# Block sums left in PSUM for the router's products, and all low weight parts of a layer made by GpSimd

## The chip, the cores and the metric

The kernel runs on one core of a Trainium2 chip. The metric is the device time of one execution in microseconds; lower is better. TensorE multiplies matrices into PSUM, VectorE and ScalarE read and write SBUF and PSUM, GpSimd works on SBUF, and SyncE (SP) issues most of the transfers.

## The reference

Linear attention feeds two layers of experts. In the attention, `q` is a softmax over its 64 columns, `k` one over the 576 rows, and the output is `q (kᵀ v)` for 8 batches of 8 heads; its rows, 4608 tokens of 512 columns, go through the two layers.

```python
def _moe_ref(x, w_skip, w_gate, w1, w2):           # first layer
    do_compute = x @ w_skip > 0
    xc = x[do_compute]; logits = xc @ w_gate
    e_idx = argmax(logits, 1); gate_w = softmax(logits)[e_idx]
    y[e] = gate_w * (relu(xc[e] @ w1[e]) @ w2[e])  # for the rows of each of 8 experts
    out[do_compute] = xc + y                       # the other rows pass unchanged
def _moe2_ref(x, emb, tau, w1, w2):                # second layer, all rows
    logits = (x / |x|) @ (emb / |emb|).T / tau
    e_idx = argmax(logits, 1); gate_w = softmax(logits)[e_idx]
    out[e] = gate_w * (relu(x[e] @ w1[e]) @ w2[e])
```

`w1` is 512x1024 and `w2` 1024x512 for each expert, in float32.

## The kernel before

The attention (up to about 200 us) ends with each token's first router; each row is scattered by an indirect DMA to a DRAM table X, sorted by expert. A plan (`Plan`, small vectors on one partition) turns the counts of rows into steps. A step is two blocks of 128 rows of one expert, or a single block at the end of an expert with an odd number of blocks. Class `Moe` holds both layers; every engine works through its instructions in the order in which they are emitted.

Each float32 product is made of three in a short format: a matrix is split into a high part (a cast on ScalarE) and a low part (matrix less high part). `split` makes the parts of an expert's weights in eight pieces of 128x512: the casts on ScalarE (L496), each low part on VectorE or GpSimd (L497) as a string of eight letters V and P says. `hilo` (L504) does the same for transposed rows, and `L1two` (L531) for the first product's output: both take one operand from PSUM and one from SBUF.

A step k of two blocks: `L1two` (L527) makes relu(x w1) for both blocks, `both` transposes the rows of step k+1 (into `pxT` and `P4[0]`; the second waits for the low half made from `P4[0]`, L531), `L2(1)` and `L2(0)` (L557) multiply by w2 into `py[1]` and `py[0]`. A single block goes through `single`. In the first layer, `done` (L563) then forms the block sum, gate times `py` plus x, in place in SBUF. `products` multiplies it with the second router's eight rows: on VectorE with a sum along the row (L625), or on GpSimd (L624) with the sum on ScalarE (`sum`, L627). `mark` (L645 to L654) finds each row's second-layer expert and adds to the counts `acc`; `before` (L664 to L667) and `rank` (L671 to L673) turn the marks into rows of X, and GpSimd scatters the two blocks there (L674).

The order of the work around a step is written out by hand. `post(k)` emits `L2(0)` and then, by the letters of `'seq': 'RGCMED'`: R the rank of step k-2, G the gates, C the next step's w1 split where the expert changes, M the mark of step k-1, E the block sum and eight products of block 1, D the block sum of block 0. `body(k)` emits `post(k-1)`, the products of block 0 (`'pre': 'PV'`: two on GpSimd, then six on VectorE), the w2 split where the expert changes, and `L1two`. The three strings `'lo'` say who makes the low parts: w2 before a step of two blocks, w2 before a single block, w1. In this run the first layer has 17 steps, of which five begin with new weights; the second layer follows from the end of the first, with its own table `PRM2`.

The layer begins (`start`) with both splits of the first expert, `plan.heads` and `plan.rows` between their pieces, and ends in `tail`, with `one` (the last mark) and `two` (counts, ranks, plan of the second layer) inside the second layer's first `L1two`.

Of the kernel before, what the change touches and what calls it, by code (L numbers as in the profile page):

```python
# [13 lines left out]
class Val:  # L14
    """Contents of one buffer of a pool, from its first writer to its last reader."""
# [6 lines left out]
class Order:  # L22
    """Orders single-engine tasks: a greedy list schedule over the engines, whose order of starts is
    the order of emission. Tasks that touch the same Val keep the order in which they were added."""
# [9 lines left out]
    def emit(self):  # L34
        last, readers = {}, {}
# [59 lines left out]
def attention(tc,nc,raw,ctx,cst,q,k,v,routers,wgt,enD,X,accF,w1,w2,early,prm={}):  # L95
    """Rows of X: x | first router's logits less their maximum | second router's products less their
    maximum | sum of squares | token | 0 | 0, sorted by layer and expert."""
    B,H,S,D=q.shape
# [30 lines left out]
    # columns that a token is multiplied with: first router, second router (rows of unit norm, over tau), skip  # L129
# [46 lines left out]
    def do_k(b):  # L176
# [34 lines left out]
        # kv = softmax(k)^T v for two heads at a time, on the diagonal blocks, and its routers' columns  # L211
# [51 lines left out]
    def do_out(b):  # L263
        # x = softmax(q) kv, tokens on the partitions
# [59 lines left out]
        # with a 0 here no expert is marked, for desc is never 0  # L324
# [28 lines left out]
    # the first expert's weights take the place of the last blocks of k and v  # L353
# [5 lines left out]
    # the first five hundred and twelve rows of expert 0, where it has that many by now  # L359
# [21 lines left out]
def consts(tc,nc,c):  # L381
    """Constants that depend on shapes only."""
# [65 lines left out]
        # end of the step's expert: the least of the ends after it  # L448
# [6 lines left out]
        # a change at the step past the end has nothing left to load  # L455
# [10 lines left out]
class Moe:  # L466
    """raw[r]: two tiles [128,2048] for layer matrix r (0: w1, 1: w2) as it came; hl: their high and low parts.
    GE: rows of a layer's first two steps; ring: of the others."""
    def __init__(self,tc,nc,sb,ps,cst,plan,raw,X,out,second,enD,acc,accE,GE,ring,flags):
        self.tc,self.nc,self.cst,self.plan,self.X,self.out,self.second,self.enD,self.acc,self.accE=tc,nc,cst,plan,X,out,second,enD,acc,accE  # L470
# [17 lines left out]
    def split(self,r,mid=(),lo='VP'*4):  # L488
        """High + low is the matrix, bit for bit, each in the short float32 format."""
# [16 lines left out]
    def val(self,r,k):  # L506
        """Row r of the plan's control at step k, loaded once."""
# [4 lines left out]
    def Tx(self,s,t,p=None):  # L512
        """Transposes a block of a step's rows; what it returns then splits them."""
# [27 lines left out]
    def Th(self,g):  # L541
        """Transposes a half of the single block's h."""
# [27 lines left out]
    def begin(self,first,mid={},then=None):  # L570
        """The first step, of two blocks, and what the second one begins with."""
# [8 lines left out]
    def late(self,first,ws):  # L580
        """The same where the first steps' rows are not here yet; the first step has one or two blocks."""
# [17 lines left out]
    def sums(self,s,n,act=False):  # L599
        """Sums of squares of the rows of n steps from s on."""  # L600
# [245 lines left out]
```

## Time and profile before

| | |
|---|---|
| Median of 3 runs | 1136.82 us (1134.54 to 1137.14) |
| Profiled execution, span from the first to the last instruction | 1129.8 us |
| What lies around the span, as median less span | 7.0 us |
| Busy: TensorE, VectorE, ScalarE, GpSimd | 987.1, 749.7, 451.0, 392.4 us |

The profiled execution has no time of its own beside its span; the median stands for it. A matmul's busy time counts from issue to a modelled end, so that a busy TensorE is not one at its peak. Times in rows are microseconds from the start of the span, unless they are marked as nanoseconds.

### The profile page before, as it was taken

What the parts mean: (1) busy time and instruction counts of PE and PEld (TensorE: products, weight loads), DVE (VectorE), ACT (ScalarE), POOL (GpSimd) and SP (SyncE); (2) the same over time, 40 slices, a digit from 0 to 9 for tenths busy, and PEclk for the clock granted to TensorE, in tenths of its full rate; (3) what the DMA queues carried; (4) which work ended last, traced back from release to release, by engine and by line L of the source; (5) the groups of instructions that cost most, each with busy time, mean ns of one, the idle gap of its engine ahead of it and who ended that gap; (6) DMA issues with size and microseconds to landing.
All of it is one profiled execution on the core that took longest, in us unless ns stands there. A gap on an engine that the chain in (4) does not pass through costs nothing. (4 is left out here: it accounts for less than half of the span.)

```text
span 1129.8 us, 19942 instructions
## 1 busy us (share of the span) xinstructions
PE 987.1 (87%) x6083; PEld 879.4 (78%) x6083; DVE 749.7 (66%) x1676; ACT 451.0 (40%) x942; POOL 392.4 (35%) x331
## 2 busy tenths in 40 slices
PE   3978788698769699796999859999999999999994
PEld 2867788586659588686998748988889899998893
DVE  4698898888988889889788882136172622264460
ACT  5657564424414116034111532335361631355352
POOL 6457453513744416316212551104141311032240
PEclk9999799699889899898999879999999999999997
DMA  9976543670551413323211127206051530042610
GB/s 275 292 224 202 197 163 116 238 229 22 188 187 47 156 59 114 116 65 135 99 55 47 43 109 249 78 20 228 30 194 50 176 115 25 25 161 73 226 38 20
DMA packets 84412, 143.71 MB, mean 127 GB/s; under 512 B 19215, under 2 KB 43791, under 8 KB 84064
## 3 DMA queue, kind: packets, MB, share of 16 engines
q1 hardware_dynamic: 74304, 114.37, 31.5%
q0 software_dynamic: 8640, 26.61, 6.2%
q8 instruction: 74, 1.21, 0.5%
q14 instruction: 146, 1.20, 0.3%
q10 hardware_dynamic: 1248, 0.32, 0.1%
HBM read 110.03 MB, written 33.68 MB: 127 GB/s over the span
## 5 line engine op out<-in xcount | busy, mean ns | idle before, releaser
L557 PE MATMUL py<-w2h,hT 128*128 128x512 f32 x1072 | 349.8, 403 | 2.8 <-DVE hT L504 2.8
L527 PE MATMUL P<-xT,w1h 128*128 128x256 f32 x1856 | 342.2, 287 | 5.2 <-DVE jk L625 2.1
L527 PEld LDWEIGHTS P<-xT,w1h 128*128 128x128 f32 x1856 | 296.1, 195 | 8.1 <-issue 6.0
L527 PE MATMUL P<-xT,w1l 128*128 128x256 f32 x928 | 266.6, 287 | 7.0 <-DVE w1l L497 6.4
L557 PEld LDWEIGHTS py<-w2h,hT 128*128 128x128 f32 x1072 | 206.6, 193 | 48.7 <-DVE hT L504 5.7
L557 PE MATMUL py<-w2l,hT 128*128 128x512 f32 x536 | 213.4, 398 | 1.4 <-DVE w2l L497 1.4
L531 DVE SCALAR_TENSOR_TENSOR hT<-P,hT 128x512 fp32r<-128x512 f32 x116 | 76.6, 685 | 183.2 <-ACT hT L530 181.8
L530 ACT ACTIVATE hT<-P 128x512 fp32r<-128x512 f32 x116 | 68.2, 595 | 302.7 <-PE P L527 302.6
L527 PEld LDWEIGHTS P<-xT,w1l 128*128 128x128 f32 x928 | 181.0, 195 | 8.0 <-DVE w1l L497 7.0
L567 POOL DMA_INDIRECT out_dram<-y,idt x38 | 38.1, 1001 | 292.5 <-ACT y L566 235.3
L557 PEld LDWEIGHTS py<-w2l,hT 128*128 128x128 f32 x536 | 103.7, 193 | 22.4 <-DVE w2l L497 1.8
L625 DVE SCALAR_TENSOR_TENSOR jk<-xb,enB 128x512 bf16<-128x512 f32 x116 | 108.1, 932 | 3.9
L497 POOL TENSOR_TENSOR w2l<-vt,w2h 128x512 fp32r<-128x512 f32 x56 | 86.8, 1579 | 2.0 <-ACT w2h L496 1.8
L497 POOL TENSOR_TENSOR w1l<-kt,w1h 128x512 fp32r<-128x512 f32 x46 | 61.3, 1362 | 61.6 <-ACT w1h L496 53.4
L566 ACT ACTIVATE y<-py,gate 128x512 f32<-128x512 f32 x38 | 26.0, 688 | 118.3 <-PE py L557 111.1
L496 ACT CAST w2h<-vt 128x512 fp32r<-128x512 f32 x104 | 56.3, 621 | 7.9 <-PE py L557 4.1
L624 POOL TENSOR_TENSOR pr<-xb,enB 128x512 f32<-128x512 f32 x20 | 34.3, 1734 | 69.2 <-DVE flag L636 66.8
L625 DVE SCALAR_TENSOR_TENSOR jk<-xg,enB 128x512 bf16<-128x512 f32 x54 | 55.5, 1028 | 1.8
L497 DVE TENSOR_TENSOR w2l<-vt,w2h 128x512 fp32r<-128x512 f32 x48 | 48.6, 1062 | 11.3 <-ACT w2h L496 8.1
L496 ACT CAST w1h<-kt 128x512 fp32r<-128x512 f32 x104 | 55.6, 640 | 0.0
L627 ACT ACTIVATE jk<-pr 128x512 bf16<-128x512 f32 x34 | 21.4, 629 | 76.3 <-POOL pr L624 75.6
L497 DVE TENSOR_TENSOR w1l<-kt,w1h 128x512 fp32r<-128x512 f32 x58 | 49.4, 908 | 1.1 <-ACT w1h L496 0.7
(260 smaller groups left out, 1481.1 us busy)
## 6 DMA issues: line engine op xcount, KB each, us to landing
vt<-in_moe_w_dram SPq DMA_DIRECT2D x26, 1024.0 KB, 7.0
kt<-in_moe_w_dram SPq DMA_DIRECT2D x26, 1024.0 KB, 7.0
xb<-X SPq DMA_DIRECT2D x56, 266.0 KB, 3.5
kt<-in_k_dram SPq DMA_DIRECT2D x16, 512.0 KB, 5.6
vt<-in_v_dram SPq DMA_DIRECT2D x16, 512.0 KB, 6.2
qt<-in_q_dram SPq DMA_DIRECT2D x8, 1024.0 KB, 8.6
xg<-X SPq DMA_DIRECT2D x28, 266.0 KB, 3.0
X<-empty SPq DMA_DIRECT2D x16, 266.0 KB, 2.3
```

What stands on the lines that cost most here:

```text
L496: nc.scalar.copy(h,a)
L497: (nc.gpsimd if lo[2*f+i]=='P' else nc.vector).tensor_tensor(out=l,in0=a,in1=h.bitcast(F32),op=ALU.subtract)
L527: T.matmul(o,lhsT=w[:,c,128*f:128*f+128],rhs=x[:,c],start=n==0,stop=n==11); n+=1
L530: A.activation(out=h,in_=q,func=AF.Relu)
L531: V.scalar_tensor_tensor(out=hl[:,f-1:f+1],in0=q,scalar=0.0,in1=h.bitcast(F32),op0=ALU.max,op1=ALU.subtract)
L557: T.matmul(self.py[t],lhsT=x[:,c,a],rhs=w[:,c],start=n==0,stop=n==23); n+=1
L566: A.activation(out=y,in_=p,func=AF.Copy,scale=gt)
L567: P.indirect_dma_start(out=self.out,out_offset=IO(self.idt[:,i:i+1]),in_=y,in_offset=None,bounds_check=NTOK-1,oob_is_err=False)
L624: for e in range(n,8) if 'P' in eng else (): self.nc.gpsimd.tensor_tensor(out=self.pr[e-n],in0=x,in1=self.enB[:,e],op=ALU.mult)
L625: for e in range(n) if 'V' in eng else (): self.nc.vector.scalar_tensor_tensor(out=self.jk,in0=x,scalar=1.0,in1=self.enB[:,e],op0=ALU.mult ...
L627: for e in range(n,8): self.nc.scalar.activation(out=self.ja,in_=self.pr[e-n],func=AF.Copy,accum_out=self.l2[s%2][:,t,e:e+1])
```

## The change

In the first layer, `done` writes the block sum over `py[t]` in PSUM, and a new ScalarE copy brings it to SBUF; `products` on VectorE reads the sum from PSUM. The small operands of `mark`, `rank` and `gates` (`m`, `pos`, `gs`, and a copy `ds` of the constant `desc`) and those of the plan (`cnt`, `en`, `w`, `odd`, `nb`, `v`, `ci`) move to the PSUM bank of `pm`, which is made a whole bank. The counts `acc` become the first of three columns of `oh`, and one reduction takes the place of two additions. The three strings `'lo'` of the first layer become `'PPPPPPPP'`. Comments are removed throughout. The core of the diff:

```diff
 class Plan:
-        self.cnt=t("cnt",[1,8]); self.ci=t("ci",[1,2,8],I32); self.nb=t("nb",[1,2,8]); self.en=t("en",[1,8]); self.w=t("w",[1,8]); self.odd=t("odd",[1,8]); self.pad=t("pad",[1,8],I32)
-        self.d=t("d",[1,NST,8]); self.v=t("v",[1,NST]); self.row=t("row",[1,2,NST],I32); self.sg=t("sg",[1,NST])
+        self.n0=t("n0",[1,8]); self.pad=t("pad",[1,8],I32)
+        self.d=t("d",[1,NST,8]); self.row=t("row",[1,2,NST],I32); self.sg=t("sg",[1,NST])
+    def bank(self,f,i):
+        self.cnt,self.en,self.w,self.odd=(f[0:1,8*k:8*k+8] for k in range(4))
+        self.nb=f[0:1,32:48].rearrange("p (a b) -> p a b",a=2); self.v=f[0:1,48:48+NST]
+        self.ci=i[0:1,0:16].rearrange("p (a b) -> p a b",a=2)
     def heads(self,base):
-        V.tensor_copy(self.nb,self.ci)
+        V.tensor_copy(self.nb,self.ci); V.tensor_copy(self.n0,self.ci[:,0])
-        V.scalar_tensor_tensor(out=self.odd,in0=m,scalar=2.0,in1=self.nb[:,0],op0=ALU.mult,op1=ALU.subtract)
+        V.scalar_tensor_tensor(out=self.odd,in0=m,scalar=2.0,in1=self.n0,op0=ALU.mult,op1=ALU.subtract)
 class Moe:
-        self.cl,=st("cl",[128,2,8]); self.m,=st("m",[128,2,2]); self.pos,=st("pos",[128,2]); self.ix=st("ix",[128,2],I32,4); self.oh=st("oh",[128,2,8],BF,2); self.l2=st("l2",[128,2,8],n=2)
+        self.cl,=st("cl",[128,2,8]); self.ix=st("ix",[128,2],I32,4); self.oh=st("oh",[128,3,8],BF,3); self.l2=st("l2",[128,2,8],n=2)
...
+        self.pv=self.pm[:,64:192]; plan.bank(self.pv[0:1,48:128],self.pm[0:1,192:208].bitcast(I32))
+        self.m=self.pv[:,0:4].rearrange("p (a t) -> p a t",a=2); self.pos=self.pv[:,4:6]; self.gs=self.pv[:,8:12]; self.ds=self.pv[:,16:32]
+        nc.vector.tensor_copy(self.ds,cst['desc'])
     def done(self,s,t,first):
             x=self.g(s)[:,t,0:512]
-            V.scalar_tensor_tensor(out=x,in0=p,scalar=gt,in1=x,op0=ALU.mult,op1=ALU.add)
+            V.scalar_tensor_tensor(out=p,in0=p,scalar=gt,in1=x,op0=ALU.mult,op1=ALU.add)
+            A.copy(x,p)
     def gates(self,s,n,first):
-            V.tensor_reduce(out=gt,in_=ex,axis=AX.X,op=ALU.add)
+            sm=self.gs[:,0:n]
+            V.tensor_reduce(out=sm,in_=ex,axis=AX.X,op=ALU.add)
-        V.tensor_scalar(out=gt,in0=gt,scalar1=1e-9,scalar2=None,op0=ALU.add)
+        V.tensor_scalar(out=gt,in0=sm,scalar1=1e-9,scalar2=None,op0=ALU.add)
     def products(self,s,t,n=8,eng='VP'):
-        for e in range(n) if 'V' in eng else (): self.nc.vector.scalar_tensor_tensor(out=self.jk,in0=x,scalar=1.0,in1=self.enB[:,e],op0=ALU.mult,op1=ALU.mult,accum_out=self.l2[s%2][:,t,e:e+1])
+        for e in range(n) if 'V' in eng else (): self.nc.vector.scalar_tensor_tensor(out=self.jk,in0=self.py[t],scalar=1.0,in1=self.enB[:,e],op0=ALU.mult,op1=ALU.mult,accum_out=self.l2[s%2][:,t,e:e+1])
     def mark(self,s):
-        V.scalar_tensor_tensor(out=self.cl,in0=sh,scalar=0.0,in1=ds,op0=ALU.is_equal,op1=ALU.mult)
+        V.scalar_tensor_tensor(out=self.cl,in0=sh,scalar=0.0,in1=self.ds.rearrange("p (t e) -> p t e",t=2),op0=ALU.is_equal,op1=ALU.mult)
-        oh=self.oh[s%2]; ac,an=self.acc[s%3],self.acc[(s+1)%3]
-        V.tensor_tensor(out=oh,in0=ds,in1=w(1),op=ALU.is_equal)
-        V.tensor_tensor(out=an,in0=ac,in1=oh[:,0],op=ALU.add)
-        V.tensor_tensor(out=an,in0=an,in1=oh[:,1],op=ALU.add)
+        oh=self.oh[s%3]
+        V.tensor_tensor(out=oh[:,1:3],in0=ds,in1=w(1),op=ALU.is_equal)
+        with nc.allow_low_precision(reason='counts of at most 36'):
+            V.tensor_reduce(out=self.oh[(s+1)%3][:,0],in_=oh.rearrange("p j e -> p e j"),axis=AX.X,op=ALU.add)
-PRM={... 'lo': ['VVVVPPPP', 'VPVPVPVP', 'VPVPVPPP'], 'pre': 'PV', 'seq': 'RGCMED', ...}
+PRM={... 'lo': ['PPPPPPPP', 'PPPPPPPP', 'PPPPPPPP'], 'pre': 'PV', 'seq': 'RGCMED', ...}
```

`before`, `rank`, `total` and the plan's `rows` change their operands' names accordingly. The string `'lot'`, for the second layer's first w2, was `'PPPPPPPP'` already, and the splits in `start` keep `'VP'*4`.

## Rows read from the trace of the kernel before

**Rows 1.** Stages: start to end us, length, busy us (instructions) of each engine, granted clock, DMA.
```profile
264.00:340.70 76.70, 56.83 (x293) 47.63 (x293) 70.70 (x129) 30.89 (x64) 42.27 (x30) 0.87 0.42 149
...
680.00:1129.80 449.80, 429.52 (x2688) 387.15 (x2686) 176.65 (x302) 181.43 (x363) 93.28 (x74) 0.98 0.32 107
```

**Rows 2.** Waits of TensorE, 200 to 690 us: total us, times, longest.
```profile
PE P L516 <- DVE hT L531: 36.4, 4, 9.6
PE pm L485 <- DVE acc L654: 11.9, 1, 11.9
...
PE P L527 <- DVE w1l L497: 6.4, 1, 6.4
```

**Rows 3.** Timeline of VectorE: start, duration, line, operation, tiles, count.
```profile
205.12 10.04 DVE L416 TENSOR_SCALAR pl_ci<-pl_cnt 1x8 int32<-1x8 f32 x2
...
358.06 6.49 DVE L646 TENSOR_TENSOR xg<-l,m 128x16 f32<-128x16 f32 x1
...
365.79 0.75 DVE L563 SCALAR_TENSOR_TENSOR xg<-py,gate,xg 128x512 f32<-128x512 f32 x1
...
385.63 2.47 DVE L531 SCALAR_TENSOR_TENSOR hT<-P,hT 128x512 fp32r<-128x512 f32 x4
...
1011.24 1.28 DVE L531 SCALAR_TENSOR_TENSOR hT<-P,hT 128x512 fp32r<-128x512 f32 x2
```

**Rows 4.** Timeline of GpSimd.
```profile
278.06 6.15 POOL L497 TENSOR_TENSOR w1l<-kt,w1h 128x512 fp32r<-128x512 f32 x5
...
303.60 0.98 POOL L674 DMA_INDIRECT X<-GE,ix  x1 [0.30 <-issue]
...
358.23 6.29 POOL L497 TENSOR_TENSOR w1l<-kt,w1h 128x512 fp32r<-128x512 f32 x5
...
437.94 6.29 POOL L497 TENSOR_TENSOR w1l<-kt,w1h 128x512 fp32r<-128x512 f32 x5
...
511.65 6.32 POOL L497 TENSOR_TENSOR w1l<-kt,w1h 128x512 fp32r<-128x512 f32 x5
...
637.16 6.31 POOL L497 TENSOR_TENSOR w1l<-kt,w1h 128x512 fp32r<-128x512 f32 x5
...
1007.78 5.95 POOL L497 TENSOR_TENSOR w2l<-vt,w2h 128x512 fp32r<-128x512 f32 x4
```

**Rows 5.** Lines 625, 531, 497: count, shortest/median/longest ns, first and last start, form.
```profile
L625 DVE SCALAR_TENSOR_TENSOR jk<-xb,enB x116: 691/693/1671, 286.5 to 625.3; 128x512 bf16<-128x512 f32 x116
...
L531 DVE SCALAR_TENSOR_TENSOR hT<-P,hT x116: 660/690/694, 222.1 to 1103.9; 128x512 fp32r<-128x512 f32 x116
...
L497 POOL TENSOR_TENSOR w2l<-vt,w2h x56: 1251/1707/1743, 210.2 to 1098.8; 128x512 fp32r<-128x512 f32 x56
```

**Rows 6.** Timeline of TensorE, with the idle time before in brackets.
```profile
340.55 0.40 PE L527 MATMUL P<-xT,w1h 128*128 128x256 f32 x2
...
364.25 0.40 PE L527 MATMUL P<-xT,w1h 128*128 128x256 f32 x2
...
386.37 1.12 PE L516 MATMUL P<-ident,xb 128*128 128x128 f32 x4 [9.64 <-DVE hT L531]
...
399.58 0.39 PE L527 MATMUL P<-xT,w1h 128*128 128x256 f32 x2
...
473.81 0.40 PE L527 MATMUL P<-xT,w1h 128*128 128x256 f32 x2
...
546.57 0.40 PE L527 MATMUL P<-xT,w1h 128*128 128x256 f32 x2
...
661.40 0.17 PE L485 MATMUL pm<-acc,ones 128*1 128x8 bf16 x1 [11.94 <-DVE acc L654]
```

**Rows 7.** Block products of two steps, columns as in rows 1.
```profile
353.20:364.40 11.20, 11.20 (x53) 9.29 (x52) 10.84 (x13) 9.51 (x18) 8.16 (x7) 1.00 0.08 21
387.10:399.70 12.60, 12.60 (x52) 10.32 (x51) 9.74 (x34) 0.71 (x2) 1.99 (x2) 0.88 0.75 253
```

**Rows 8.** Line 566: count, shortest/median/longest ns, first and last start, form.
```profile
L566 ACT ACTIVATE y<-py,gate x38: 681/688/690, 679.2 to 1115.1; 128x512 f32<-128x512 f32 x38
```

More of the change, by code (lines that the diff above doesn't have):

```diff
@@ L466, with __init__ @@
 class Moe:
-    def __init__(self,tc,nc,sb,ps,cst,plan,raw,X,out,second,enD,acc,accE,GE,ring,flags):
-        self.tc,self.nc,self.cst,self.plan,self.X,self.out,self.second,self.enD,self.acc,self.accE=tc,nc,cst,plan,X,out,second,enD,acc,accE
+    def __init__(self,tc,nc,sb,ps,cst,plan,raw,X,out,second,enD,accE,GE,ring,flags):
+        self.tc,self.nc,self.cst,self.plan,self.X,self.out,self.second,self.enD,self.accE=tc,nc,cst,plan,X,out,second,enD,accE
         self.GE,self.flags=GE,flags; self.sent={}; self.fresh()
@@ L662, in before @@
         T,cst=self.nc.tensor,self.cst
-        p=self.below(s); oh=self.oh[s%2]
-        T.matmul(p,lhsT=cst['tri'],rhs=oh,start=True,stop=False)
+        p=self.below(s); oh=self.oh[s%3]
+        T.matmul(p,lhsT=cst['tri'],rhs=oh[:,1:3],start=True,stop=False)
         T.matmul(p,lhsT=cst['ones1'],rhs=cst['base'][:,8:16].unsqueeze(1).to_broadcast([1,2,8]),start=False,stop=False)
-        T.matmul(p,lhsT=cst['ones'],rhs=self.acc[s%3].unsqueeze(1).to_broadcast([128,2,8]),start=False,stop=False)
-        T.matmul(p[:,1],lhsT=cst['ones'],rhs=oh[:,0],start=False,stop=True)
+        T.matmul(p,lhsT=cst['ones'],rhs=oh[:,0:1].to_broadcast([128,2,8]),start=False,stop=False)
+        T.matmul(p[:,1],lhsT=cst['ones'],rhs=oh[:,1],start=False,stop=True)
     def rank(self,s,last=False):
         V,P=self.nc.vector,self.nc.gpsimd
-        t=self.g(s); oh=self.oh[s%2]; ix=self.ix[s%4]; p=self.below(s)
+        t=self.g(s); oh=self.oh[s%3][:,1:3]; ix=self.ix[s%4]; p=self.below(s)
         V.tensor_tensor(out=self.cl,in0=p,in1=oh,op=ALU.mult)
@@ L774, in tail @@
             if k==0:
-                self.split(0); self.split(1); self.total(self.acc[0]); self.arrange(False,gdeps); plan.rest(False); self.late(False,after); return
+                self.split(0); self.split(1); self.total(self.oh[0][:,0]); self.arrange(False,gdeps); plan.rest(False); self.late(False,after); return
             n=PRM['nt']
@@ L779, in two @@
                 S=range(max(0,k-2),k)
-                self.total(self.acc[k%3],[lambda s=s: self.before(s) for s in S])
+                self.total(self.oh[k%3][:,0],[lambda s=s: self.before(s) for s in S])
                 for s in S: self.rank(s,True)
@@ L803 @@
 PRM2={'pre': '', 'sum': -1, 'bef': -1, 'chg': 1, 'lo': ['VPVPVPVP', 'VPPPVPPP', 'VVPVVVPV'], 'seq': 'CGED'}
-PRM={'nt': 6, 'lot': 'PPPPPPPP', 'f0': 6, 'f1': 4, 'f2': 7, 'nd': 6, 'sum': 6, 'bef': 5, 'chg': 1, 'lo': ['VVVVPPPP', 'VPVPVPVP', 'VPVPVPPP'], 'pre': 'PV', 'seq': 'RGCMED', 'early': 6, 'step': 10.176829472231454, 'win': 0.1, 'fine': {0: 2, 7: 2, 3: 2, 2: 2, 4: 2, 1: 2, 5: 2, 6: 2}, 'bufs': {'eq': 3, 'ek': 2, 'kt': 2, 'qt': 2, 'vp': 3, 'vt': 2, 'xb': 2}, 'kV': (3, 7), 'qV': (7,), 'nA': (0, 2, 3, 4, 6, 7), 'off': {'k': -6.484502494166867, 'v': 11.118172098269266, 'q': 28.85943784881458, 'K': 7.166893295536811, 'O': 18.45975243148315, 'S': 50.0}, 'tail': (6, 7), 'ob': {'v5': 5.954492296568429, 'v7': 7.221793060578019, 'q3': 2.159865636021178, 'S4': 3.8269400797246447, 'v4': -4.865487979166696, 'k2': -0.0410587724241839, 'v0': -2.1047421268295925, 'q7': -2.0142255377528797, 'k1': 1.2850377249193103, 'q2': -8.327514905478694, 'K4': -1.2765299453962793, 'O0': 0.6553924136789928, 'v1': 7.255343197815394, 'k0': 4.502663169702918, 'q6': -0.3041990385917977, 'S5': -1.484286947528986, 'K0': 3.4420525242401063, 'v2': -0.6325078913282336, 'K7': 4.831269581125951, 'S2': -0.6137849008016073, 'k4': -0.035399030020154806, 'K6': 1.0230510413508602, 'v6': 2.730442247511302, 'O7': 0.37053874544361565, 'S7': 0.4782436340656335, 'O6': 2.9398983585308587, 'K5': 0.4290589715182519}}
@@ new lines @@
+PRM={'nt': 6, 'lot': 'PPPPPPPP', 'f0': 6, 'f1': 4, 'f2': 7, 'nd': 6, 'sum': 6, 'bef': 5, 'chg': 1, 'lo': ['PPPPPPPP', 'PPPPPPPP', 'PPPPPPPP'], 'pre': 'PV', 'seq': 'RGCMED', 'early': 6, 'step': 10.176829472231454, 'win': 0.1, 'fine': {0: 2, 7: 2, 3: 2, 2: 2, 4: 2, 1: 2, 5: 2, 6: 2}, 'bufs': {'eq': 3, 'ek': 2, 'kt': 2, 'qt': 2, 'vp': 3, 'vt': 2, 'xb': 2}, 'kV': (3, 7), 'qV': (7,), 'nA': (0, 2, 3, 4, 6, 7), 'off': {'k': -6.484502494166867, 'v': 11.118172098269266, 'q': 28.85943784881458, 'K': 7.166893295536811, 'O': 18.45975243148315, 'S': 50.0}, 'tail': (6, 7), 'ob': {'v5': 5.954492296568429, 'v7': 7.221793060578019, 'q3': 2.159865636021178, 'S4': 3.8269400797246447, 'v4': -4.865487979166696, 'k2': -0.0410587724241839, 'v0': -2.1047421268295925, 'q7': -2.0142255377528797, 'k1': 1.2850377249193103, 'q2': -8.327514905478694, 'K4': -1.2765299453962793, 'O0': 0.6553924136789928, 'v1': 7.255343197815394, 'k0': 4.502663169702918, 'q6': -0.3041990385917977, 'S5': -1.484286947528986, 'K0': 3.4420525242401063, 'v2': -0.6325078913282336, 'K7': 4.831269581125951, 'S2': -0.6137849008016073, 'k4': -0.035399030020154806, 'K6': 1.0230510413508602, 'v6': 2.730442247511302, 'O7': 0.37053874544361565, 'S7': 0.4782436340656335, 'O6': 2.9398983585308587, 'K5': 0.4290589715182519}}
@@ L810, in model @@
         X=tc.dram_tile([ZROW+128,XW],F32,name="X"); enD=tc.dram_tile([8,512],F32,name="enD")
-        wgt=c.tile([128,4,17],F32,name="wgt"); accF=c.tile([128,16],BF,name="accF"); acc=[c.tile([128,8],BF,name=f"acc{i}") for i in range(3)]
+        wgt=c.tile([128,4,17],F32,name="wgt"); accF=c.tile([128,16],BF,name="accF")
         flags=[c.tile([1,1],I32,name=f"flag{i}") for i in range(4)]; [nc.gpsimd.memset(x,0) for x in flags[1:3]]; GE=c.tile([128,4,XW],F32,name="GE")
@@ L818, in model @@
         sb=ctx.enter_context(tc.tile_pool(name="m_sb",bufs=1)); ps=ctx.enter_context(tc.tile_pool(name="m_ps",bufs=1,space=PSUM))
-        m=Moe(tc,nc,sb,ps,cst,plan,wt,X,out,wgt[:,:,8:16],enD,acc,accF[:,0:8],GE,xb,flags)
-        nc.gpsimd.tensor_copy(acc[0],accF[:,8:16])
+        m=Moe(tc,nc,sb,ps,cst,plan,wt,X,out,wgt[:,:,8:16],enD,accF[:,0:8],GE,xb,flags)
+        nc.gpsimd.tensor_copy(m.oh[0][:,0],accF[:,8:16])
         m.layer(True,(m1w1,m1w2),(m2w1,m2w2),0,scat)
```

7 lines of the change are left out of this document (4 added, 3 removed).

## Prediction

> **What bounds the kernel now.** I read the profile from coarse to fine. The table of stages first: in the second layer (680 us to the end) TensorE is busy 95% of the time and VectorE 39%; in the first layer's stretch from 264 to 340.7 us TensorE is busy 74% and VectorE 92% [rows 1]. So something is to be won in the first layer, and VectorE is the engine to suspect. Then the waits of TensorE in that layer: the largest end with a VectorE instruction, 36.4 us in four waits of up to 9.6 us for the low half of hT, 11.9 us for the class counts, 6.4 us for a low weight part [rows 2]. VectorE's own timeline through one of the long waits shows why it is late: the subtraction at L646, over 128x16 elements, lasts 6.49 us, and the low halves that TensorE waits for come out only at 385.63 us [rows 3]; between them stand the products at L625, whose durations run from 691 to 1671 ns [rows 5]. Last, L646 is laid beside GpSimd: it begins just before GpSimd's run of five low parts (358.23 us, 6.29 us) and ends with it [rows 3, 4], and it reads nothing that GpSimd makes. The plan's two instructions at L416, over 1x8, take 10.04 us at the start [rows 3].
>
> **What lets VectorE go.** The products read two operands from SBUF. The low halves at L531 read one from PSUM and one from SBUF; all 116 take 660 to 694 ns [rows 5], and two of them, at 1011.24 us, lie inside a GpSimd run that lasts from 1007.78 to 1013.7 [rows 3, 4]. The change gives the first layer's products, marks and plan an operand in PSUM, so I price them like the low halves, and GpSimd's parts beside them at their undisturbed pace: 6.29 / 5 = 1.26 us (6.15 to 6.32 in the other runs of five [rows 4]); the median of all w2 parts is 1707 ns [rows 5].
> The Trainium skill (SBUF — State Buffer, Who interferes with whom) says that a VectorE instruction with two SBUF inputs contends with a GpSimd instruction that reads SBUF, and that one with at most one SBUF input, outside the two-port modes, doesn't. The trace agrees, with 1671 against 694 ns; by that rule the sum below stands, without it the third rival's.
>
> **The change part by part.**
> VectorE sheds three things: the stalls of 198 products (693 ns each without one), that of L646, and 38 low parts (seven at each of five changes of expert, three at the end; the start keeps its eight). At the change at 358 us its queue then reads: mark at 357.9 us, some 1.4 us (the six small instructions behind L646 take 1.2, from 364.55 to 365.79 [rows 3]); the first block sum, 0.75 us, once TensorE has it at 358.7 (364.25 [rows 6] less the other block's 5.6, half of 11.2 [rows 7]); eight products at 0.74 us with their accumulator reads, to 365.4; second block sum and six products, to 370.7; first low half at 371 to 372.5 us instead of 385.63. TensorE wants it from 376.7 on (386.37 less 9.64 [rows 6]): this wait goes, with 4 us to spare.
> Added on ScalarE: 29 copies from PSUM to SBUF, 0.69 us each by the nearest row [rows 8], on an engine busy 40% of the time from 264 to 340.7 us [rows 1]. They lie beside VectorE's products. If the products have to wait for the copy as well (both read one bank; no row shows whether), a change pays 2 x 0.7 us out of the 4 us to spare: still nothing on the path; with that cover gone up to 1.4 us a change. GpSimd's two products wait 0.7 us for the copy, but last 1.3 instead of some 1.7: even. TensorE doesn't meet the longer hold of py: its next use of it stands behind low halves that VectorE makes after the products.
> The merged counts save one small instruction a step, off the path.
> Added on GpSimd: 38 low parts at 1.26 us. Behind a single block they come on the path. GpSimd's queue at a change is eight w1 parts, two products, eight w2 parts; behind its last part TensorE still has 0.3 us of that block and 5.6 us of the last one. In order:
> - Start: the 6.4 us wait ends, because the plan's heads no longer stand 10 us before the third low part. Behind a long wait the granted clock is 0.88 against 1.00, and the block products last 12.6 instead of 11.2 us [rows 7]: 1.4 us return too. Gain 7.8.
> - Two changes in a row from 278.06 us: 32 parts and 4 products at 1.26 and two scatters at 1.3 (0.98 and 0.30 between [rows 4]) are 47.9 us; GpSimd is done at 326.0, the step at 331.9 instead of 340.55 [rows 6]. Gain 8.6.
> - Change at 358 us: the w1 parts are made from 358.23 to 368.3, ahead of their use from 364.25 on; the w2 parts end at 380.9, needed at about 382 (376.7 and seven eighths of 5.6). The step takes the 23.7 us of an undisturbed one (340.55 to 364.25) instead of 35.3 [rows 6]. Gain 11.6.
> - Changes behind single blocks, from 437.94 and 511.65 us: 18 operations, 22.7 us, and 5.9: 466.5 against 473.81, 540.3 against 546.57 [rows 4, 6]. Gains 7.3 and 6.3.
> - End: w1 parts from 637.16 [rows 4] to 647.2, two products to 649.8, ScalarE's sum to 650.6, mark to 652.1; the counts stand at 661.40 now [rows 6]. 9.3 us, and 1.4 of slow clock. The eight w2 parts end at 659.8, just before the block product wants the last, some 8 us after the counts. SP's writes of empty rows follow the counts and come forward with them. Gain 10.7.
> Sum 52.3 us. The second layer keeps its instructions and starts earlier by all of it. Span 1129.8 - 52.3 = 1077.5; the median of the runs shown is 7.0 us above that span, which I leave as it is: 1084.5.
>
> **Bounds of what no row shows.** A low part on GpSimd beside the new forms: 1.25 to 1.74 us [rows 5]; I take 1.26, for the row nearest to it is the run beside L531's form, 5.95 us for four with some SBUF work in it [rows 4]. Each 0.1 us more costs 3.6 us in the double change, 1.8 at each single one, 0.5 at 358 us and 1.0 at the end: 8.7. A block sum written to PSUM: 0.75 us, at most the 0.7 of a second pass more, inside the 4 us. The last four scatters now end near 666 us (661.4 and four at 1.3), then near 665, while the second layer's use of those rows comes forward by 10.7: nothing if they have 9 us to spare, 9 us late if none; I take nothing, for no wait for them is among the large ones.
>
> **Rivals.** First, GpSimd slower than its own rows, since casts, scatters and products meet in one queue: at 1.45 us a part 17 us of the gain go, 1101. For it: its chain is the bound in four of five changes. Against it: its runs of five have no gaps. The Trainium skill (GPSIMD Engine Reference, Engine selection) sends two-input elementwise work to VectorE, as about twice as fast. The trace agrees (1.26 against about 0.69 us); if all 38 parts lay on the path, that were 38 x 0.57 = 22 us, and 1106.
> Second, something else is late in VectorE's place, the rows of the second layer or ScalarE's copies behind its casts: 5 to 10 us in all, 1092. Against it speak the 4 us to spare.
> Third, on the other side: the stall isn't one of operands, GpSimd stays at 1.71 us a part and VectorE at its present pace. The double change then ends at 348 us (7.6 us later than now), the single ones 0.8 and 1.8 later; L646 waits for eight parts instead of five, and nothing else is gained: 1147. It decides once products from PSUM show 1.6 us beside GpSimd. Against it stand the 694 ns of L531.
> Fourth, the seams eat all of it: 1137. No row speaks for it.
>
> **How the numbers follow.** Forecast (1074 to 1090) 0.60; second rival (1088 to 1098) 0.12; first (1095 to 1110) 0.16; better than 1074, if the slow clock at the later steps goes too, 0.03; third 0.06; fourth 0.03. Predicted 1084.5. Without the third, the fourth, the best and the slowest of the first: 1072 to 1107. Faster by over 0.3% (what a measurement here tells from none) 0.91, same 0.03, slower 0.06.
>
> **What would show it.** Right: no product of the first layer and no L646 over 0.75 us; the 9 us waits before the second transpose gone; low parts in runs of eight of 10.1 us; new waits of TensorE for GpSimd's w1l and w2l, some 20 us in all, most between 278 and 326; the wait for the counts down to about 3 us. Wrong: products of 1.6 us; low parts over 1.4; TensorE waiting for ScalarE's copy or for the second layer's rows.

## The result

Over four runs of each the changed kernel takes 1091.0 us (1089.65 to 1094.19) against 1135.7 us (1133.91 to 1137.14): ratio 0.9613, 95% interval 0.9594 to 0.9632. Predicted were 1084.5 us, 1072 to 1107. The profiled execution has a span of 1088.5 us and took 1090.26 us; the span forecast was 1077.5.

Line numbers have moved: L497, L527, L531, L516, L557, L625, L646 of before are now L506, L536, L540, L525, L566, L638, L659; the new copy is L574. Stages first, columns as in [rows 1] (the layer begins 4.4 us later here than before):

```profile
206.00:264.00 58.00, 50.07 (x299) 45.58 (x298) 43.56 (x111) 19.20 (x38) 15.50 (x16) 0.87 0.57 205
264.00:340.70 76.70, 66.94 (x355) 54.44 (x354) 44.59 (x136) 34.32 (x70) 55.59 (x46) 0.93 0.43 149
...
640.00:1088.50 448.50, 428.04 (x2688) 386.25 (x2688) 176.35 (x302) 182.06 (x364) 94.16 (x74) 0.98 0.32 108
```

From 264 to 340.7 us VectorE's busy time has fallen from 70.70 to 44.59 us, and TensorE's has risen from 56.83 to 66.94: in the same length it does 355 instructions instead of 293. The second layer is as it was. TensorE's waits, 200 to 640 us (total us, times, longest):

```profile
PE P L536 <- DVE w1l L506: 5.3, 1, 5.3
PE P L553 <- ACT h L549: 5.1, 5, 1.7
PE P L536 <- POOL w1l L506: 4.5, 5, 2.4
...
PE py L566 <- POOL w2l L506: 3.3, 12, 0.3
PE P L548 <- POOL w1l L506: 3.1, 2, 2.7
PE pm L494 <- DVE oh L668: 2.9, 1, 2.9
```

The 36.4 us for the low half of hT [rows 2] are gone from the first layer, and the wait for the counts is 2.9 us instead of 11.9. One line of before is still there, nearly as long: 5.3 us for a low part of w1 at the start. Single lines of VectorE and ScalarE (shortest/median/longest ns):

```profile
L638 DVE SCALAR_TENSOR_TENSOR jk<-py,enB x198: 691/691/693, 241.5 to 613.1; 128x512 bf16<-128x512 f32 x198
...
L659 DVE TENSOR_TENSOR xg<-l,pm x5: 170/171/171, 350.8 to 619.9; 128x16 f32<-128x16 f32 x5
...
L506 DVE TENSOR_TENSOR w1l<-kt,w1h x40: 669/682/8732, 208.9 to 1044.1; 128x512 fp32r<-128x512 f32 x40
...
L574 ACT COPY xb<-py x17: 586/587/588, 282.9 to 589.7; 128x512 f32<-128x512 f32 x17
```

No product and no L659 stalls any more ([rows 5] had 1671 ns, [rows 3] 6.49 us). But a VectorE low part of 8732 ns has appeared. Its place, in the timeline of VectorE at the start:

```profile
209.55 0.35 DVE L421 TENSOR_SCALAR pm<-pm 1x8 int32<-1x8 f32 x2
...
211.38 8.73 DVE L506 TENSOR_TENSOR w1l<-kt,w1h 128x512 fp32r<-128x512 f32 x1
220.04 0.18 DVE L433 TENSOR_TENSOR pl_d<-pm,step 1x40 f32<-1x40 f32 x1
```

and in that of GpSimd, at the start and in the double change:

```profile
209.66 5.00 POOL L506 TENSOR_TENSOR w1l<-kt,w1h 128x512 fp32r<-128x512 f32 x4
214.63 4.93 POOL L506 TENSOR_TENSOR w2l<-vt,w2h 128x512 fp32r<-128x512 f32 x4
...
306.49 9.97 POOL L506 TENSOR_TENSOR w1l<-kt,w1h 128x512 fp32r<-128x512 f32 x8
316.43 2.53 POOL L637 TENSOR_TENSOR pr<-xb,enB 128x512 f32<-128x512 f32 x2
318.92 10.01 POOL L506 TENSOR_TENSOR w2l<-vt,w2h 128x512 fp32r<-128x512 f32 x8
```

The plan's 10.04 us [rows 3] are 0.35, but the third low part behind them (VectorE's second), which reads both its operands from SBUF, now begins at 211.38 and ends at 220.11, just behind GpSimd's run (219.56). A run here is a row of GpSimd instructions with no gap between them. The stall has moved on to the next such instruction.

Of the two L416 instructions of before only the second waited, 9.96 us, to the end of GpSimd's run; it reads one tensor from SBUF and writes SBUF, so two SBUF inputs are not the only form that waits. Where TensorE begins a step's first product (columns as in [rows 6]):

```profile
208.78 0.55 PE L536 MATMUL P<-xT,w1h 128*128 128x256 f32 x1 [1.14 <-issue]
243.99 0.47 PE L536 MATMUL P<-xT,w1h 128*128 128x256 f32 x2 [1.45 <-DVE jk L638]
335.13 0.40 PE L536 MATMUL P<-xT,w1h 128*128 128x256 f32 x2
358.79 0.40 PE L536 MATMUL P<-xT,w1h 128*128 128x256 f32 x2
382.46 0.40 PE L536 MATMUL P<-xT,w1h 128*128 128x256 f32 x2
449.39 0.40 PE L536 MATMUL P<-xT,w1h 128*128 128x256 f32 x2
516.04 0.40 PE L536 MATMUL P<-xT,w1h 128*128 128x256 f32 x2
621.15 0.17 PE L494 MATMUL pm<-oh,ones 128*1 128x8 bf16 x1 [2.85 <-DVE oh L668]
```

The first is the layer's first product, at 204.35 us in the trace of before, the second the next step's, 240.38 there; the others answer to [rows 6]. The gaps between neighbours give each term's size, below.

### The profile page after: what moved, and what is told of

Its sections match the earlier page's. It is cut to its first block, busy times and chain, and to the rows that moved or that the text cites. A ratio compares the mean times of both kernels' runs of the same rounds, so it can differ in the third digit from the quotient of the medians.

```text
span 1088.5 us, 19924 instructions
## 1 busy us (share of the span) xinstructions
PE 984.2 (90%) x6083; PEld 872.4 (80%) x6083; DVE 632.7 (58%) x1624; ACT 466.7 (43%) x971; POOL 413.9 (38%) x369
## 5 line engine op out<-in xcount | busy, mean ns | idle before, releaser
L536 PE MATMUL P<-xT,w1h 128*128 128x256 f32 x1856 | 345.4, 288 | 5.1 <-ACTq L722 2.3
L566 PE MATMUL py<-w2h,hT 128*128 128x512 f32 x1072 | 343.6, 396 | 2.7 <-issue 2.4
L536 PEld LDWEIGHTS P<-xT,w1h 128*128 128x128 f32 x1856 | 298.3, 197 | 8.3 <-issue 3.6
L536 PE MATMUL P<-xT,w1l 128*128 128x256 f32 x928 | 267.9, 289 | 9.8 <-DVE w1l L506 5.3
L566 PEld LDWEIGHTS py<-w2h,hT 128*128 128x128 f32 x1072 | 201.6, 189 | 46.6 <-DVE hT L513 3.7
L566 PE MATMUL py<-w2l,hT 128*128 128x512 f32 x536 | 211.3, 394 | 4.4 <-POOL w2l L506 3.3
L540 DVE SCALAR_TENSOR_TENSOR hT<-P,hT 128x512 fp32r<-128x512 f32 x116 | 77.7, 687 | 213.4 <-ACT hT L539 204.3
L536 PEld LDWEIGHTS P<-xT,w1l 128*128 128x128 f32 x928 | 182.3, 196 | 11.6 <-POOL w1l L506 5.5
L638 DVE SCALAR_TENSOR_TENSOR jk<-py,enB 128x512 bf16<-128x512 f32 x198 | 136.9, 691 | 24.3 <-ACT xb L574 10.7
L566 PEld LDWEIGHTS py<-w2l,hT 128*128 128x128 f32 x536 | 101.2, 189 | 32.9 <-POOL w2l L506 10.3
L506 POOL TENSOR_TENSOR w1l<-kt,w1h 128x512 fp32r<-128x512 f32 x64 | 84.2, 1344 | 59.9 <-ACT w1h L505 51.8
L506 POOL TENSOR_TENSOR w2l<-vt,w2h 128x512 fp32r<-128x512 f32 x76 | 101.8, 1368 | 1.4 <-issue 0.8
L290 PE MATMUL po<-KV,eT 128*128 128x164 f32 x256 | 48.6, 342 | 11.7 <-DVE xr L298 9.0
L290 PEld LDWEIGHTS po<-KV,eT 128*128 128x128 f32 x256 | 42.3, 216 | 13.4 <-DVE xr L298 9.5
L574 ACT COPY xb<-py 128x512 f32<-128x512 f32 x17 | 10.0, 587 | 96.9 <-DVE flag L649 50.6
L348 POOL DMA_INDIRECT X<-xb,pi x32 | 33.1, 1035 | 44.1 <-ACT pi L343 35.5
L513 DVE TENSOR_TENSOR hT<-P,hT 128x512 fp32r<-128x512 f32 x18 | 12.4, 687 | 63.8 <-ACT hT L512 63.8
```

The source lines that it names most:

```text
L290: T.matmul(po.tile[:,c,0:CW],lhsT=eT.tile[:,c] if g is None else eT.tile[:,g,c],rhs=kv.tile[:,c],start=n==0,stop=n==len(ins)-1)
L348: i=P.indirect_dma_start(out=X,out_offset=IO(pi.tile[:,j:j+1]),in_=xt()[:,j],in_offset=None,bounds_check=ZROW,oob_is_err=False)
L506: (nc.gpsimd if lo[2*f+i]=='P' else nc.vector).tensor_tensor(out=l,in0=a,in1=h.bitcast(F32),op=ALU.subtract)
L513: self.nc.vector.tensor_tensor(out=l,in0=p,in1=h.bitcast(F32),op=ALU.subtract)
L536: T.matmul(o,lhsT=w[:,c,128*f:128*f+128],rhs=x[:,c],start=n==0,stop=n==11); n+=1
L540: V.scalar_tensor_tensor(out=hl[:,f-1:f+1],in0=q,scalar=0.0,in1=h.bitcast(F32),op0=ALU.max,op1=ALU.subtract)
```

## The experiments

The attention ahead of the change varies from run to run (its end lay between 196.5 and 213.8 us), so each profile is also read from the first layer's first transposition (201.17 us before, 205.59 after) to the end. That part repeats: 882.9 and 882.1 us in two runs of the changed kernel. The last column is the first layer alone, from its first product to the product that makes the counts. What lies behind the counts takes 464.2 to 468.4 us in all runs but e11, though no other edit touches it; why it varies wasn't traced, so a few microseconds of a difference in the column to the end can come from there. Each ratio is to runs of before made beside that kernel; their medians are 1135.7 us (changed), 1129.8 (e1 to e4), 1134.2 (e5, e6, e7, e9) and 1126.0 (e8, e10, e11, e12), so a median is compared only within its group.

| kernel | median us | ratio to before, 95% interval | first transposition to end, us | first product to counts, us |
|---|---|---|---|---|
| before | 1135.7 | 1 | 928.6 | 457.1 |
| changed | 1091.0 | 0.9613 (0.9594 to 0.9632) | 882.9 | 412.4 |
| e1 operands only | 1097.9 | 0.972 (0.9654 to 0.9785) | 894.1 | 423.5 |
| e2 parts only | 1138.9 | 1.0083 (1.005 to 1.0115) | 936.2 | 468.8 |
| e3 products from SBUF | 1156.6 | 1.0237 (1.02 to 1.0273) | 954.2 | 484.0 |
| e4 start on VectorE | 1076.7 | 0.9514 (0.9477 to 0.9552) | 875.1 | 406.1 |
| e5 marks in SBUF | 1099.9 | 0.9695 (0.9655 to 0.9734) | 892.1 | 423.1 |
| e6 eight products on VectorE | 1079.5 | 0.9509 (0.947 to 0.9548) | 872.2 | 404.8 |
| e7 e4 and e6 | 1076.1 | 0.9494 (0.9463 to 0.9526) | 867.8 | 398.6 |
| e8 start on GpSimd | 1081.1, one run | | 877.0 | 407.7 |
| e9 changed again | 1091.7 | 0.9622 (0.9588 to 0.9656) | 882.1 | 412.4 |
| e10 before, start on VectorE | 1123.1, one run | | 919.9 | 449.2 |
| e11 e7, second layer's parts on GpSimd | 1082.2 | 0.9598 (0.9564 to 0.9632) | 881.3 | 396.7 |
| e12 e7 with seven products | 1069.6 | 0.9512 (0.9459 to 0.9566) | 868.0 | 398.7 |

### The two halves of the change apart

e1 keeps the operands and puts the strings of before back:
```diff
-'lo': ['PPPPPPPP', 'PPPPPPPP', 'PPPPPPPP']
+'lo': ['VVVVPPPP', 'VPVPVPVP', 'VPVPVPPP']
```


> The changed kernel with the three strings of low parts as they were before: only the operands in PSUM, the block sum's copy and the merged counts are kept. Theory 1 (two SBUF inputs on VectorE are what waits for GpSimd, and both halves of the change are needed): the products take 0.69 us and L659, the old L646, 0.17 us, but VectorE's own low parts have two SBUF inputs and stand beside GpSimd's runs, so single ones of them last 3 to 6 us; half to three quarters of the gain stays, 1100 to 1115 us. Theory 2 (the gain comes from taking low parts off VectorE's queue, whatever the operands): 1125 us or more, little better than before. Theory 3 (the operands alone do it): 1088 to 1095 us, as the whole change.

e2 makes the opposite edit in the kernel before.

> The kernel before with nothing changed but the three strings: all low parts of a layer on GpSimd, products and marks still with two operands in SBUF. Theory 1: VectorE loses its own parts, but its products last up to 1.67 us beside longer GpSimd runs, GpSimd's parts about 1.7 us beside the products, and L646 waits for a run of eight, about 10 us instead of 6.5: 1130 to 1150 us, no gain or a loss. Theory 2: 1090 to 1100 us. Theory 3: 1130 us or more as well.

The operands alone give 34.5 of the 45.7 us; the parts alone cost 7.6 (11.7 up to the counts); on top of the operands the same parts give 11.2. Of the three theories the first holds. Theory 2, which wanted e1 at 1125 us or more and e2 at 1090 to 1100, falls by both medians. e1's median, 1097.9 us, lies between the ranges of theories 1 and 3; theory 3 falls by the 11.2 us, and by VectorE's own low parts, which wait in e1. The first of the three here lasts 7.22 us, up to the end of GpSimd's run:

```profile
282.86 8.42 DVE L506 TENSOR_TENSOR w2l<-vt,w2h 128x512 fp32r<-128x512 f32 x3
```
```profile
284.58 4.95 POOL L506 TENSOR_TENSOR w2l<-vt,w2h 128x512 fp32r<-128x512 f32 x4
```

TensorE waits 15.2 us in four times for the low half behind such parts. What the strings do to a product with two SBUF inputs, in e2's timelines of VectorE and GpSimd:

```profile
305.45 22.59 DVE L625 SCALAR_TENSOR_TENSOR jk<-xb,enB 128x512 bf16<-128x512 f32 x1 [0.48 <-DVE flag L636]
```
```profile
305.19 9.96 POOL L497 TENSOR_TENSOR w1l<-kt,w1h 128x512 fp32r<-128x512 f32 x8
315.13 2.54 POOL L624 TENSOR_TENSOR pr<-xb,enB 128x512 f32<-128x512 f32 x2
317.63 9.86 POOL L497 TENSOR_TENSOR w2l<-vt,w2h 128x512 fp32r<-128x512 f32 x8
```

One product waits for 18 GpSimd instructions, until the last ends at 327.5; two more products last 21.20 and 9.08 us, and three additions of the counts (L653, L654) 10.5 to 10.7. GpSimd loses less: the median of its w2 parts is 1.29 us, but 16 of the first layer's 52 last 1.70 to 1.74, beside products of about 1.63. The expectation had named 1.67 us a product and 1.7 a part; both occur, but it had not foreseen a product that waits for a whole run, which is the longest wait.

### Which operands

e3 gives the products their SBUF operand back, behind the copy; e5 the small operands of the marks alone:
```diff
-in0=self.py[t],scalar=1.0,in1=self.enB[:,e]
+in0=x,scalar=1.0,in1=self.enB[:,e]
```


> The changed kernel, but VectorE's products read the block sum from SBUF, after ScalarE's copy; marks, plan and strings stay changed. Theory 1: products up to 1.67 us beside GpSimd, GpSimd's median part up from 1.26 to 1.5 or 1.7 us, and GpSimd's queue is what bounds the changes of expert: 38 parts by up to 0.45 are 17 us, and VectorE's later low halves come on top: 1105 to 1125 us. Rival (only the tiny instructions with two SBUF inputs were worth something, the products' stalls cost nothing on the path): 1089 to 1095 us.

```diff
+pvs,=st("pvs",[128,48])
-self.m=self.pv[:,0:4]...; self.pos=self.pv[:,4:6]; self.gs=self.pv[:,8:12]; self.ds=self.pv[:,16:32]
+self.m=pvs[:,0:4]...; self.pos=pvs[:,4:6]; self.gs=pvs[:,8:12]; self.ds=pvs[:,16:32]
```


> The changed kernel with only the small operands of mark, rank and gates (m, pos, gs, ds) back in SBUF; products from PSUM, plan in PSUM, all parts on GpSimd. Theory 1 (any VectorE instruction with two SBUF inputs, however small, waits until GpSimd's run ends): L659 stands just behind the start of a run of eight and lasts up to 10 us; the first low half is late by 10 less 4 us to spare at the change in step 6 and like it at the others: 10 to 25 us from first transposition to end, and the counts' wait up by up to 8: 1100 to 1117 us. Rival (only large operands matter; small reads slip in between): within 2 us of the changed kernel.

e3 costs 71 us, far over the 14 to 34 expected: products of 20.88, 19.20, 21.25, 20.94 and 19.29 us stand at five changes (8.4 at the one in step 6), each up to the end of GpSimd's chain of w1 parts, products and w2 parts, here the first:

```profile
278.64 20.88 DVE L638 SCALAR_TENSOR_TENSOR jk<-xb,enB 128x512 bf16<-128x512 f32 x1 [0.65 <-ACT xb L574]
```
```profile
289.13 9.84 POOL L506 TENSOR_TENSOR w2l<-vt,w2h 128x512 fp32r<-128x512 f32 x8
```

GpSimd's parts keep a mean of 1.29 and 1.30 us, so its queue was not what suffered. e5 costs 10.7 us up to the counts, at the low end of the 10 to 25 expected (9.2 to the end); 8.2 of it is TensorE's wait for the counts, 11.1 us instead of 2.9. Lines of e5:

```profile
L659 DVE TENSOR_TENSOR xg<-l,pvs x5: 174/176/8809, 350.9 to 621.8; 128x16 f32<-128x16 f32 x5
...
L666 DVE TENSOR_TENSOR oh<-desc,pvs x17: 174/175/10612, 259.2 to 631.3; 128x16 bf16<-128x16 f32 x17
...
L687 DVE TENSOR_TENSOR ix<-pvs,xg x5: 161/163/5854, 373.8 to 633.7; 128x2 int32<-128x2 f32 x5
```

Most instances take 0.17 us; one that falls into a run lasts 4.4 to 10.6 us, with two elements a partition as with sixteen. Which instance falls in is a matter of microseconds: at the change in step 6 none did here, as two scatters kept GpSimd's run back until the mark was done.

### The start

e4 puts the first expert's sixteen parts on VectorE, e8 on GpSimd, e10 on VectorE in the kernel before:
```diff
-self.split(0,(lambda: plan.heads(...),lambda: plan.rows(8*AREA,0,5)))
+self.split(0,(lambda: plan.heads(...),lambda: plan.rows(8*AREA,0,5)),'V'*8)
-self.split(1)
+self.split(1,(),'V'*8)
```


> The changed kernel with all sixteen low parts of the first expert on VectorE instead of every other one. In the changed kernel VectorE's third part lasts 8.73 us at the start, until GpSimd's run of eight ends, and TensorE waits 5.29 us for it. Theory 1 (it is the same stall, moved from the plan to the low part behind it): with no GpSimd run beside it every part lasts 0.65 us, the 5.3 us wait goes, with up to 1.4 us of slow clock: 1084 to 1087 us. Rival (VectorE becomes late with twice the parts, or the wait only moves to the second product): 1089 to 1095 us.

> The changed kernel with all sixteen low parts of the first expert on GpSimd, VectorE keeping the plan alone. Theory 1 (VectorE's third part was late only because it has two SBUF inputs beside a run): GpSimd's third and fourth part come out 5.0 us after its start, as TensorE gets to them, and its last 20.1 us after it, before TensorE wants that one: 874 to 877 us from the first transposition to the end, as with all parts on VectorE (875.1). Rival (a part takes twice as long on GpSimd, and the start is bound by whoever makes them): 879 us or more.

> The kernel before with nothing changed but the sixteen low parts of the first expert, all on VectorE; the plan's operands stay in SBUF. Theory 1 (the plan's 10.04 us were a wait for GpSimd's run of eight, and with no run there is none, whatever the operands): the two instructions of L416 take 0.2 us each, the 6.4 us wait goes, 920 to 922 us from the first transposition to the end instead of 928.6. Rival (the plan's instructions are slow by themselves with operands in SBUF): 927 us or more.

All three came out on theory 1's side: 875.1, 877.0 and 919.9 us, e10 just under its range; e8 and e10 are one run each. e4's median, 1076.7 us, is below the 1084 to 1087 expected; from the first transposition it gains 7.8 us, where the expectation's 5.3 and 1.4 make 6.7; the group of runs is a faster one besides (before takes 5.9 us less in it). VectorE in e4, then in e10:

```profile
211.19 2.48 DVE L506 TENSOR_TENSOR w1l<-kt,w1h 128x512 fp32r<-128x512 f32 x4
213.59 4.89 DVE L506 TENSOR_TENSOR w2l<-vt,w2h 128x512 fp32r<-128x512 f32 x8
```
```profile
206.09 0.23 DVE L416 TENSOR_SCALAR pl_ci<-pl_cnt 1x8 int32<-1x8 f32 x2
```

With no run beside them the parts take 0.62 us, and the plan's 10.04 us are 0.23 with their operands in SBUF: at the start the PSUM operands were not needed, the mixture of two engines was the cause. The rival, an L416 that is slow by itself, falls too. From the first product to the next step's, before takes 36.0 us, the changed kernel 35.2, e4 28.4.

### One run more, and the attention

> The changed kernel once more, as the measure for the others of this call and for how far one kernel's runs differ: 1088 to 1094 us. From the first layer's first transposition to the end 882.9 us, whatever the attention ahead of it takes (199.4 to 205.6 us in the runs so far).

The measure repeats, and the attention is one reason why medians wander: it ended at 205.6 and 209.6 us in two runs of one kernel. In the changed kernel's trace its longest VectorE instruction is of the same kind, beside GpSimd instructions that follow one another from 102.56 to 113.45 us:

```profile
104.28 9.25 DVE L321 TENSOR_TENSOR xb<-ls,rt 128x64 f32<-128x64 f32 x1
```
In the trace of before the same instruction got in sooner, between two GpSimd instructions:
```profile
107.00 2.87 DVE L321 TENSOR_TENSOR xb<-ls,rt 128x64 f32<-128x64 f32 x1
```

Of the fourteen profiles six show about 9 us here and eight 2.9; the attention ends on average at 206 us in the six and 201 in the eight, and both groups hold kernels made from the one before and from the changed one. That this one wait makes all of the difference isn't shown.

### GpSimd's queue

e6 takes the first block's two products off GpSimd, e7 does it with e4's start, e12 leaves one; e11 carries the strings of the first layer into the second, on e7:
```diff
-PRM={... 'nd': 6, ...}
+PRM={... 'nd': 8, ...}
```


> The changed kernel with all eight products of the first block on VectorE as well (six before, two on GpSimd with their sums on ScalarE). Theory 1 (GpSimd's queue now bounds the changes behind single blocks and the double one; VectorE has room): GpSimd sheds 2.6 us a block, of TensorE's waits for GpSimd's parts (11 us) 5 to 9 us go: 1082 to 1086 us. Rival (VectorE's two products more, 1.5 us a step, make its low halves late, or the scatters set GpSimd's pace): within 2 us of the changed kernel, or above it.

> The changed kernel with both: sixteen low parts of the first expert on VectorE, and all eight products of both blocks on VectorE. The start gave 7.7 us from the first transposition to the end; with the 5 to 9 us expected of the products 866 to 871 us from there to the end, 1068 to 1075 us in all. Rival (the products give nothing): 875 us, as with the start alone.

> The kernel with sixteen parts on VectorE, and seven of the first block's products there, one on GpSimd (six and two gave 875.1 us from the first transposition to the end, eight and none 867.8, with a new wait of TensorE of 4.7 us for VectorE's products). If GpSimd's queue is what counts, each product costs half of the 7.3 us: 870 to 873 us. If VectorE's products are a second bound by now, the middle is the best: 864 to 867 us.

```diff
-PRM2={... 'lo': ['VPVPVPVP', 'VPPPVPPP', 'VVPVVVPV'], ...}
+PRM2={... 'lo': ['PPPPPPPP', 'PPPPPPPP', 'PPPPPPPP'], ...}
```


> The kernel with sixteen parts and all products on VectorE, and the second layer's low parts all on GpSimd too. It takes 466.0 us from the counts to the end now. Theory 1, carried over (VectorE's parts with two SBUF inputs last 1.3 to 1.7 us beside GpSimd's): little hangs on it, for TensorE is busy 95% there: 462 to 466 us. Rival (GpSimd's queue, with two scatters of output a step in it, is late with w1 and w2): 468 to 476 us.

e6 gives 10 us to the end but 7.6 up to the counts, inside the 5 to 9 expected, and e7 as much beyond e4 (7.5; to the end 867.8). TensorE's weight loads (PEld) waited 10.3 us for GpSimd's w2 parts in the changed kernel and 3.9 in e6; their 6.3 us for ScalarE's output h [L549] are gone as well. ScalarE's sums of GpSimd's two products (L640) had waited 17.5 us for these products and stood in the same queue as h. So GpSimd's queue was a bound of the changes, by its parts and, through the sums, by ScalarE; the two shares weren't separated. Then VectorE becomes another, in e7's waits of TensorE:

```profile
PE P L536 <- POOL w1l L506: 5.8, 8, 2.4
PE py L566 <- DVE jk L638: 4.7, 3, 1.6
```

e12 loses that 4.7 us wait and still takes 868.0, neither of its two expectations. No single wait stands in its place: the weight loads wait 6.2 us for GpSimd's w2 parts instead of 2.4 and 3.1 for ScalarE's high half of hT, and less for others. e7 and e12 beat both kernels of the change, e7 by 15.6 us in the group of runs that it shares with the changed one (1076.05 against 1091.69). e11 fails: 481.4 us from the counts to the end instead of 466.0, worse than the rival's 468 to 476. Its waits, 640 us to the end:

```profile
PE py L566 <- POOL w2l L506: 3.7, 12, 0.7
PE py L566 <- ACT y L577: 3.0, 1, 3.0
PE py L566 <- POOLq L722: 2.5, 6, 0.7
PE P L548 <- POOLq L722: 2.1, 1, 2.1
```

These are TensorE waiting for GpSimd's parts, for ScalarE's output and at branches that GpSimd reaches late; they add up to 11.3 us. From the counts to the end the waits are 13.5 us in e11 and 8.4 in e7, where none is for GpSimd. The weight loads show it more plainly: in e11 they wait 10.1 us for GpSimd's w2 parts and 7.6 at those branches, in e7 for neither. TensorE's busy time is 10 us longer besides, at a granted clock of 0.97 instead of 0.98. How far the one follows from the other is open.

e11 also shows a second instruction with one SBUF input that waits: L628, a TENSOR_SCALAR over 128x4 from SBUF to SBUF, lasts 4.26 us up to the end of a GpSimd run, and 0.15 to 0.17 without one.

## Why the prediction was right, and where it wasn't

Each term from the gaps between steps, before less after:

| term | predicted | measured |
|---|---|---|
| start | 7.8 | 36.03 - 35.21 = 0.8 |
| double change | 8.6 | 100.17 - 91.14 = 9.0 |
| change in step 6 | 11.6 | 35.33 - 23.67 = 11.7 |
| behind the single blocks | 7.3 and 6.3 | 7.3 and 6.1 |
| end | 10.7 | 114.83 - 105.11 = 9.7 up to the counts, 1.1 behind |
| sum | 52.3 | 45.7 |

**The step that failed is the start.** It said that the 6.4 us wait ends, "because the plan's heads no longer stand 10 us before the third low part". The heads no longer stand there; but the third part is itself a VectorE instruction with two SBUF inputs beside the same GpSimd run, and takes the stall over: 8.73 us, and TensorE's wait is 5.3. I had applied the rule to the instructions that the change edits and not to the one queued behind them. e4 shows the term itself well sized, 7.6 us, and e10, in one run, that 8.0 are to be had with nothing of the change.

**The operands.** Right: 691 to 693 ns for all 198 products, 0.17 for marks, no wait for hT left in the first layer. The Trainium skill (SBUF — State Buffer, Who interferes with whom) lets a VectorE instruction contend with GpSimd when it has two SBUF inputs or runs in a two-port mode, which a tensor_scalar can enter. The traces of e1, e2, e3 and e5 agree for two inputs. L416 and L628 are tensor_scalar instructions with one; whether they ran in such a mode no trace shows. The prediction took L416 for one case with the others. The Trainium skill tells in the same place of a lock for the length of an instruction. Here the wait lasted for up to 18 of them (22.59 us).

**GpSimd's pace.** Right: runs of eight last 9.96 to 10.06 us (10.1 said), and the double change's chain, from 281.63 to 328.93, 47.3 us (47.9). No part of the changed kernel's first layer lasts over 1.32 us, so neither the first rival's 1.45 us nor the third's 1.71 occurs there. Where the products keep two SBUF inputs some do last that long (16 of 52 w2 parts in e2, four in e3, 1.70 to 1.74 us), as the third rival had it. e2 is that rival's nearest trial and comes out slower than before, as it said, by 7.6 us; its longest waits, though, are VectorE's, up to 22.59 us.

**New waits.** TensorE's matmuls wait 10.9 us for GpSimd's w1l and w2l; its weight loads, which the profile lists apart, wait 19.6 (10.3 for w2l, 5.5 and 3.8 for w1l), and these are the 20 of the prediction, half of them in the double change. For the counts 2.85 us, as said (3). The copies take 0.587 us (0.69 said); the products do wait for them, 18.5 us of VectorE's time in 29 times, and TensorE for products once, 1.4 us: inside the 4 us to spare. By the profile that wait ends with the copy and has nothing to do with GpSimd. No loss in the second layer's rows: 467.3 us from the counts to the end, 468.4 before. So the median, 1091.0 us, lies above the forecast's band (1074 to 1090) and in the second rival's (1088 to 1098), but neither of the two things that this rival named was late.

**What lies around the span.** I took 7.0 us as lying around it; a run shows 1090.26 - 1088.5 = 1.8. By this the profiled execution of before took an estimated 1131.6 us, less than any timed one. Span 1088.5 against 1077.5 forecast is 11.0 off: 6.6 of the sum, and 4.4 by which the attention ended later in this run. In the median the 5.2 us of the wrong offset cancel half of that, and the median lies 0.7 above the profiled execution, so that 1084.5 was 6.5 off. That is about the start's 7.0 us, but by luck: without the cancelling the forecast would have been some 12 us too low.

**Engine choice.** The Trainium skill (GPSIMD Engine Reference, Engine selection) would leave two-input elementwise work to VectorE. The trace agrees for the products (e6: 7.6 us up to the counts) and the second layer (e11), and differs in the first layer's changes, where the parts on GpSimd are worth 11.2 us (e1 against the changed kernel).

## What to carry to other kernels

When a stall beside GpSimd is taken from a VectorE instruction, look at the next one of its kind in the same queue: it can inherit the wait unless GpSimd's run goes too. Either keep every VectorE instruction with two SBUF inputs out of GpSimd's back-to-back runs, whatever its size, and a TENSOR_SCALAR from SBUF to SBUF too (L416, L628), or give the whole piece of work to one engine (e4, e8). Count the wait, at worst, by the length of GpSimd's run and not by the instruction's own time.

## What was not expected of the hardware

- A VectorE instruction with two SBUF inputs waited for a whole unbroken run of GpSimd: 8.73 us (the rest of a run of eight), 10.61 us for 128x16, 5.85 us for 128x2, 22.59 us behind 18 instructions. GpSimd kept 1.25 to 1.29 us a part.
- A VectorE TENSOR_SCALAR with one SBUF input waited in the same way: 9.96 us for 1x8 (L416) and 4.26 for 128x4 (L628).
- Elsewhere the two take turns, as here in the second layer of e7, VectorE's timeline and then GpSimd's:

```profile
717.15 4.78 DVE L506 TENSOR_TENSOR w2l<-vt,w2h 128x512 fp32r<-128x512 f32 x3 [0.41 <-ACT w2h L505]
```
```profile
716.69 6.38 POOL L506 TENSOR_TENSOR w2l<-vt,w2h 128x512 fp32r<-128x512 f32 x4 [0.39 <-issue]
```

Three VectorE parts take 1.6 us each and four GpSimd parts as well, where alone they take 0.62 and 1.26. The 1707 ns of [rows 5] are of this kind: in the kernel before 38 of the 56 w2 parts on GpSimd last 1.70 to 1.74 us, 24 of them in the first layer beside products of 1.63 to 1.68. What decides between turns and waiting wasn't settled; L321 got in after 2.87 us in one run and 9.25 in another.
